# Step one's transform: products in the order of its weights, results two apart in PSUM, and a spectrum with 32 channels in a row

## The chip, the cores and the metric

The kernel runs on one core of one Trainium2 chip. The metric is the device time of one execution in microseconds (us); lower is better. The core has five engines with queues of their own: TensorE (PE, with its weight loads shown apart as PEld), VectorE (DVE), ScalarE (ACT), GpSimd (POOL) and SyncE (SP, which here only issues transfers). SBUF is the working memory, PSUM the memory into which TensorE writes its products; both have 128 partitions. All numbers in this kernel are 32-bit floats of 4 bytes.

## The reference, cut to what matters

```python
# x = A_q [1, 2048, 640]; sa, ca, ga, sb, cb, gb = parts of silu(c) @ w_mod
def _A_ref(q, k, v, shift_k, ssm_k, ssm_D):
    k_pad = jnp.pad(k, ((0, 0), (ks - 1, 0), (0, 0)))
    for t in range(ks):                       # ks = 4: short convolution
        k_shift = k_shift + k_pad[:, t:t + S, :] * shift_k[:, ks - 1 - t][None, None, :]
    kv = k_shift * v
    # long causal convolution of kv with ssm_k, channel by channel, by FFT of length 2 S
    y = irfft(rfft(kv padded) * rfft(ssm_k padded))[:S]
    y = y + kv * ssm_D[None, None, :]
    return q * y

h = _layernorm(x, axis=-1) * (1 + ca) + sa
x = x + ga * _A_ref(h, A_k, A_v, A_shift_k, A_ssm_k, A_ssm_D)
h = _layernorm(x, axis=-1) * (1 + cb) + sb
x = x + gb * _B_ref(h, B_w1, B_b1, B_w2, B_b2)   # MLP across the 2048 tokens
```

S is 2048 tokens and D is 640 channels. The change touches the first half alone, the long convolution inside `_A_ref`.

## The kernel before

**Two halves.** From the start to about 310 us the kernel computes the first half, by channels: five blocks `c` of 128 channels (`DC`, `NC`). The rest of the span is the token MLP, matrix products of 320 columns (lines 432, 1026, 951), which the change doesn't touch.

**One block of channels.** A block holds 128 channels as 2 times 64 (the two halves of the partitions, `h`), and the 2048 tokens as 64 times 32 (`n1` times `n2`). The transform over tokens is made in two steps, with matrices as constants.

- *The short convolution* (`kv_ops`, in four groups `g` of 8 `n2`): multiplications and additions, mostly on DVE, with one group in three of the first blocks on POOL. The last operation multiplies by `v` and writes the product tile `X`, 128 x 2048. Before the change X lies in the order (n2, channel): the 64 channels of one `n2` in a row. The block after the present one is convolved while the present one is transformed (the list `fill`, taken off by `dv(n)`).
- *The filter* comes by transfer into `KSR` (tile `aux`), and `perm` on ACT brings it into `KSP` (tile `p`), where the 64 values of one pair of channels lie in a row.
- *Step one* (`step1(side, t)`, matmuls at line 218): side 0 is X, side 1 is the filter. A call takes 8 pairs of channels, each with two matmuls (`ri`, real and imaginary, into the two halves of the partitions of PSUM). The pair's 128 x 64 values are the weights, and the constant `F1`, 128 columns, is the moving operand. For the filter these weights lie in a row; for X they are 32 elements (128 bytes) apart. Each matmul writes 128 columns in a row to PSUM. ACT then moves the call's 1024 columns to the spectrum `Z` (tile `z`, line 220). A block has four calls for each side.
- *Step two* (`f2(g)`, matmuls at line 234, eight calls of 32 matmuls in a block): weights from the constant `W2`, 64 in a row; the moving operand is one frequency's 64 columns of `Z`, which lie as 32 runs of two elements, 256 elements (1024 bytes) apart. ACT copies the filter's half (line 238), DVE multiplies (two operations), POOL adds into `Y`.
- *The way back*: `i2` (line 263; ACT moves the results to `T2` by line 271), `i1` (line 282; its moving operand is read from `T2` in runs of two elements, 512 bytes apart), then `gate` on DVE and POOL.

**What sets the order.** The order on every engine is the order in which the program is written (`manual_schedule`). PE's results go to a ring of three PSUM tiles of 1024 columns (`psum`), so a call can start when the third last has been read out. In blocks 1 to 3 the calls for the next block's X stand between this block's `i2` and `i1`, and those for the next filter after the first `i1`. Two matmuls that write different halves of the partitions can run at one time.

A 32-bit matmul is two instructions on PE, each with a weight load of its own, so a call of step one shows as 32 matmuls and 32 weight loads, and a call of step two as 64.

## Time and profile before

| | |
|---|---|
| median of 3 runs | 719.09 us (716.91 to 719.27) |
| the profiled execution | 718.91 us, of which the profiled span is 716.8 us |
| mean granted TensorE clock | 0.985 of full speed |
| PE busy | 646.4 us, 90% of the span |
| DVE, ACT, POOL busy | 487.0, 296.9, 118.4 us |
| step one, matmuls on X | 640 instructions, 44.8 us busy |
| step one, matmuls on the filter | 640 instructions, 39.4 us busy |
| step two, matmuls | 2560 instructions, 95.7 us busy |
| ACT, PSUM to spectrum | 40 instructions of 1140 ns |

The span is what lies between the first and the last instruction of the profile; the execution's own time is 2.1 us longer. Matmuls overlap, so an instruction's mean duration is longer than the distance from one to the next; the distance is busy time through count. Of a wait the profile names the releaser that came last.

### The profile page before, as it was taken

Reading aid. Unit: us, or ns where it says so; the run is one execution under the profiler, and the core shown is the slowest. Engines: PE = TensorE matmul, PEld = TensorE weight load, DVE = VectorE, ACT = ScalarE, POOL = GpSimd, SP = SyncE. Lnnn points to the kernel's source line nnn. Section 1 sums busy time; section 2 is a strip of 40 time slices with the busy share of each in tenths; the row PEclk is TensorE's granted clock in tenths of the full one; section 3 lists DMA queues with packets and bytes.
Section 4 is the critical chain, followed back from the end, with each engine's and each line's share of the span. In section 5 each row is a group of like instructions: output and inputs, shape, how many; then the busy total and the mean of one; then the engine's idle time right before and its main releaser. Section 6 shows DMA issues by size and latency. Waiting matters only on the chain.

```text
span 716.8 us, 20779 instructions
## 1 busy us (share of the span) xinstructions
PE 646.4 (90%) x9131; PEld 624.4 (87%) x9131; DVE 487.0 (68%) x861; ACT 296.9 (41%) x465; POOL 118.4 (17%) x135
## 2 busy tenths in 40 slices
PE   0699677989999989988799999999999989999997
PEld 0699457989999979777799999999999989999997
DVE  7768448969879538888885223112489778888887
ACT  0534373645745636456666223113244222333231
POOL 5183028414324126000110000000000000000000
PEclk9999999999999999999999999999999999999999
DMA  9978988527243522361203633443253523455510
GB/s 184 242 222 229 387 150 165 131 47 158 54 84 90 169 62 63 112 149 31 59 1 59 118 60 60 91 86 59 75 169 104 152 89 122 129 167 168 157 48 37
DMA packets 167184, 84.90 MB, mean 118 GB/s; under 512 B 89235, under 2 KB 157622, under 8 KB 167094
## 3 DMA queue, kind: packets, MB, share of 16 engines
q1 hardware_dynamic: 162546, 82.27, 45.5%
q10 hardware_dynamic: 4548, 1.31, 1.1%
q8 instruction: 71, 1.16, 0.7%
q14 instruction: 19, 0.16, 0.1%
HBM read 73.07 MB, written 10.49 MB: 117 GB/s over the span
## 4 chain that ended last, share of the span: by engine, by line
PE 54%; DVE 22%; DMA 8%; ACT 5%; SPq 5%; issue 4%; POOL 0%; ACTq 0%; DVEq 0%
PE pst L432 21%; PE pst L234 9%; PE pst L218 8%; PE pst L1026 7%; PE pst L263 4%; DVE m_w L59 4%; SPq L495 3%; DVE m_x L59 3%; PE pst L282 2%; DMA aux<-in_A_ssm_k_dram 2%; ACT m_w L939 2%; PE pst L951 2%; DMA aux<-in_w_mod_dram 2%; DVE m_x L960 1%; DVE m_v L59 1%
## 5 line engine op out<-in xcount | busy, mean ns | idle before, releaser
L234 PEld LDWEIGHTS pst<-z,w 128*64 128x64 f32 x2560 | 94.7, 141 | 7.7 <-ACT z L220 7.3
L234 PE MATMUL pst<-z,w 128*64 128x64 f32 x2560 | 95.7, 240 | 6.2 <-ACT z L220 6.1
L218 PE MATMUL pst<-v,x 128*64 128x128 f32 x640 | 44.8, 298 | 24.1 <-DVE x L59 24.0
L220 ACT ACTIVATE z<-pst 128x1024 f32<-128x1024 f32 x40 | 45.6, 1140 | 49.3 <-PE pst L218 30.2
L59 DVE TENSOR_TENSOR p<-pst,kt 128x512 f32<-128x512 f32 x80 | 51.4, 685 | 21.2 <-ACT kt L238 13.4
L218 PEld LDWEIGHTS pst<-v,x 128*64 128x64 f32 x640 | 42.8, 221 | 24.8 <-POOL t L457 23.4
L59 POOL TENSOR_TENSOR y<-p 128x256 f32<-128x256 f32 x72 | 55.2, 800 | 43.4 <-DVE p L59 43.3
L238 ACT ACTIVATE kt<-pst 128x512 f32<-128x512 f32 x40 | 25.1, 628 | 52.6 <-PE pst L234 31.9
L830 ACT ACTIVATE pst<-pst,sm 128x640 f32<-128x640 f32 x14 | 10.7, 767 | 86.0 <-PE pst L432 85.9
L951 PE MATMUL pst<-r_z,m_w 128*128 128x320 f32 x222 | 43.1, 313 | 3.0 <-DVE m_w L59 2.5
L218 PE MATMUL pst<-v,p 128*64 128x128 f32 x640 | 39.4, 281 | 6.5 <-DVE aux L59 4.6
L218 PEld LDWEIGHTS pst<-v,p 128*64 128x64 f32 x640 | 36.8, 141 | 7.8 <-DVE aux L59 4.8
L263 PEld LDWEIGHTS pst<-v,y 32*128 32x128 f32 x1280 | 37.7, 187 | 3.1 <-issue 1.6
L939 ACT ACTIVATE m_w<-m_v 128x896 fp32r<-128x896 f32 x24 | 22.1, 948 | 42.8 <-DVE m_v L59 31.0
L263 PE MATMUL pst<-v,y 32*128 32x64 f32 x1280 | 39.2, 272 | 0.6 <-ACT z L220 0.6
L951 PEld LDWEIGHTS pst<-r_z,m_w 128*128 128x128 f32 x222 | 34.8, 188 | 4.9 <-DVE m_w L59 4.0
L59 DVE TENSOR_TENSOR tap<-tap,kt 128x512 f32<-128x512 f32 x51 | 35.5, 696 | 1.3
L59 DVE TENSOR_TENSOR kt<-in,tap 128x512 f32<-128x512 f32 x51 | 35.0, 686 | 1.4
L59 DVE TENSOR_TENSOR m_w<-m_v,m_w 128x896 fp32r<-128x896 f32 x24 | 26.0, 1087 | 10.5 <-ACT m_w L939 10.5
L282 PEld LDWEIGHTS pst<-z,v 64*64 64x64 f32 x1280 | 24.8, 158 | 7.6 <-issue 4.3
L282 PE MATMUL pst<-z,v 64*64 64x64 f32 x1280 | 26.5, 244 | 5.2 <-issue 2.9
L939 ACT ACTIVATE m_w<-m_p 128x896 fp32r<-128x896 f32 x12 | 11.4, 952 | 47.1 <-DVE m_p L59 40.7
(277 smaller groups left out, 1421.0 us busy)
## 6 DMA issues: line engine op xcount, KB each, us to landing
x<-in_B_w_dram SPq DMA_DIRECT2D x22, 512.0 KB
m_v<-in_B_w_dram SPq DMA_DIRECT2D x15, 384.0 KB
x<-in_B_w_dram SPq DMA_DIRECT2D x14, 384.0 KB
aux<-in_A_ssm_k_dram SPq DMA_DIRECT2D x10, 512.0 KB
in<-in_A_k_dram SPq DMA_DIRECT2D x36, 128.0 KB
in<-in_A_v_dram SPq DMA_DIRECT2D x36, 128.0 KB
m_x<-xs SPq DMA_DIRECT2D x28, 160.0 KB
out_dram<-m_x SPq DMA_DIRECT2D x28, 160.0 KB
```

The lines of the kernel that those rows point to most:

```text
L59: TT = lambda eng, o, a, b, op: eng.tensor_tensor(o, a, b, op=op)
L218: pe.matmul(ps[64 * ri:64 * ri + 64, o:o + 128], lhs, F1[:, 128 * ri:128 * ri + 128], start=True, stop=True)
L220: evac = lambda: act.activation(Z[:, side, t].rearrange("p a k e -> p e a k"), ps.rearrange("p (e a k) -> p e a k", a=8, e=2), AF.Copy)
L234: pe.matmul(ps[64 * h:64 * h + 64, o:o + 64], W2[k1 // 32][:, 2 * (k1 % 32) + ri], rhs, start=True, stop=True)
L238: act.activation(kt.rearrange("p (m i) -> p m i", i=32), pv[:, :, 1], AF.Copy)
L263: pe.matmul(pp[qd // 2][:, o:o + 64], Y[p, ri, i:i + 2].rearrange("p i k -> p (i k)"), V2[p, 64 * ri:64 * ri + 64], start=ri == 0, stop=ri ...
L282: pe.matmul(ps[64 * b:64 * b + 64, 512 * e + 64 * jj:512 * e + 64 * jj + 64], V1[p, ri, n2], T2[p, :, 32 * ri + n2], start=ri == 0, stop=r ...
L432: pe.matmul(ps[0:m, h, 0:320], w_.bitcast(F32R), r_[:, 320 * h:320 * h + 320].bitcast(F32R), start=first and i == 0, stop=last and i == 2)
L495: sync.dma_start(XH[j // 8][64 * b:64 * b + 64, j % 8], dram(q, (16 * b + j) * D, [[32 * D, 64], [1, D]]))
L939: act.activation(W[n][0].bitcast(F32R), a(w_), AF.Copy)
L951: pe.matmul(bank[n], w[:, i].bitcast(F32R), r.bitcast(F32R), start=i == 0 and k == 0, stop=i == 6 and k == 2)
L1026: pe.matmul(acc[s][:, h, 0:320], w[:, f_].bitcast(F32R), u[r + h].bitcast(F32R), start=f_ == 0 and k == 0, stop=f_ == NF - 1 and k == 2)
```

## The change

Four things are changed together; none of them adds or takes away an instruction, a transfer or a wait, and the order on every engine is the same.

- The last product of the short convolution writes X in the order (pair of channels, n2, channel of the pair), so that the weights of one call's matmul, 64 elements, lie in a row. Each write is then a run of two elements, and the next run is 64 elements (256 bytes) further. The two channels of a pair are now neighbours (2 i and 2 i + 1) where they were 32 apart, and `perm` reads the filter in this order too.
- Step one's matmuls write every second element of PSUM (`o:o + 255:2`), so that two pairs of channels interleave.
- ACT reads PSUM in a row and writes `Z` in runs of two elements, 32 elements (128 bytes) apart. Before, it read PSUM in a row too and wrote single elements 2 elements (8 bytes) apart. The constant `F1` has its columns in another order for this.
- Step two reads its 64 columns as two runs of 32 elements. The readers behind it (`T2` in `i2`, `gate`) follow the new order of channels.

```diff
-    f1 = np.zeros((2, 64, 2, 2, 64))
+    f1 = np.zeros((2, 64, 2, 64, 2))
...
-        f1[h, :, 0, h], f1[h, :, 1, h] = np.cos(a), np.sin(a)
+        f1[h, :, 0, :, h], f1[h, :, 1, :, h] = np.cos(a), np.sin(a)
...
-    Z = T_z.rearrange("p (s t a k e) -> p s t a k e", s=2, t=4, a=8, e=2)
+    Z = T_z.rearrange("p (s k t a e) -> p s t a k e", s=2, k=128, t=4, e=2)
...
     def perm(c):
         act.activation(KSP.rearrange("p i (n e) -> p i e n", e=2),
-                       KSR.rearrange("p (e i n) -> p i e n", e=2, i=32), AF.Copy)
+                       KSR.rearrange("p (i e n) -> p i e n", e=2, i=32), AF.Copy)
...
     def kv_ops(g, eng=dve):
...
+        pairs = lambda t: t.rearrange("p n (i e) -> p n i e", e=2)
...
-        ops.append(lambda: TT(eng, X.rearrange("p (n i) -> p n i", i=64)[:, 8 * g:8 * g + 8], S_,
-                              VX[:, 8 * g:8 * g + 8], ALU.mult))
+        ops.append(lambda: TT(eng, X.rearrange("p (i n e) -> p n i e", i=32, e=2)[:, 8 * g:8 * g + 8],
+                              pairs(S_), pairs(VX[:, 8 * g:8 * g + 8]), ALU.mult))
...
     def step1(side, t, later=False):
...
-            lhs = KSP[:, i] if side else X.rearrange("p (m i) -> p i m", i=32)[:, i]
-            o = 512 * (a % 2) + 128 * (a // 2)
+            lhs = KSP[:, i] if side else X.rearrange("p (i m) -> p i m", i=32)[:, i]
+            o = 256 * (a // 2) + a % 2
             for ri in range(2):
-                pe.matmul(ps[64 * ri:64 * ri + 64, o:o + 128], lhs, F1[:, 128 * ri:128 * ri + 128], start=True,
+                pe.matmul(ps[64 * ri:64 * ri + 64, o:o + 255:2], lhs, F1[:, 128 * ri:128 * ri + 128], start=True,
                           stop=True)
-        evac = lambda: act.activation(Z[:, side, t].rearrange("p a k e -> p e a k"),
-                                      ps.rearrange("p (e a k) -> p e a k", a=8, e=2), AF.Copy)
+        evac = lambda: act.activation(Z[:, side, t], ps.rearrange("p (a k e) -> p a k e", a=4, e=2), AF.Copy)
...
     def f2(g):
...
-                    rhs = bass.AP(tensor=T_z.tensor, offset=T_z.offset + 128 * h + 2 * k1,
-                                  ap=[T_z.ap[0], [256, 32], [1, 2]])
+                    rhs = bass.AP(tensor=T_z.tensor, offset=T_z.offset + 64 * k1 + 32 * h,
+                                  ap=[T_z.ap[0], [4096, 2], [1, 32]])
...
     def i2(r, eng=None):
...
-            o = T2[:, 8 * qd + 4 * r:8 * qd + 4 * r + 4].rearrange("p a m e -> p a e m")
-            i = pp[qd // 2][:, 512 * (qd % 2):512 * (qd % 2) + 512].rearrange("p (a e m) -> p a e m", a=4, e=2)
+            a = 16 * (qd // 2) + 8 * r
+            o = T2[:, a:a + 8, :, qd % 2]
+            i = pp[qd // 2][:, 512 * (qd % 2):512 * (qd % 2) + 512].rearrange("p (a m) -> p a m", a=8)
...
     def gate(c, ps, half, eng=pool, j0=0, j1=8, then=()):
...
-        av = a.rearrange("p j (m e) -> p e j m", e=2)
-        TT(dve, av, ps.rearrange("p (e j m) -> p e j m", e=2, j=8)[:, :, j0:j1], av, ALU.mult)
+        av = a.rearrange("p j (y e c) -> p e (j y) c", e=2, c=2)
+        TT(dve, av, ps.rearrange("p (e y c) -> p e y c", e=2, c=2)[:, :, 32 * j0:32 * j1], av, ALU.mult)
```

## The prediction, as it was put on record before the changed kernel ran

> **What bounds the kernel now.** I read the chain of waits first, for where a faster or slower step would move the end. Its columns are start, length (us) and what ran.
>
> ```profile
> 70.93 11.49 DMA aux<-in_w_mod_dram
> 82.46 1.31 PE tap L342 x12
> 84.48 14.87 DMA aux<-in_A_ssm_k_dram
> ...
> 111.01 5.41 PE pst L218 x64
> 116.44 1.10 ACT z L220
> ...
> 137.19 4.27 PE pst L218 x64
> 141.46 3.73 PE pst L263 x128
> 145.19 2.24 PE pst L218 x32
> ...
> 161.89 5.42 PE pst L218 x96
> 167.39 1.09 ACT z L220
> 168.53 19.03 PE pst L234 x507
> ```
>
> Up to 111 us the end hangs on transfers (the rows of 11.49 and 14.87 us). From there to about 300 us it runs through PE: step one (L218), one ACT copy (L220), step two (L234), the way back (L263, L282), block after block. The windows confirm it (length, PE, PEld, DVE, ACT, POOL busy, granted clock, DMA share, GB/s):
>
> ```profile
> 60.20:82.50 22.30, 16.83 (x284) 13.56 (x287) 18.39 (x56) 10.50 (x14) 3.47 (x5) 0.92 0.93 304
> 111.00:116.40 5.40, 5.38 (x64) 5.14 (x64) 5.16 (x8) 1.12 (x1) 5.17 (x5) 0.68 0.94 164
> 116.40:137.20 20.80, 19.48 (x514) 19.14 (x514) 18.37 (x30) 10.88 (x22) 13.38 (x15) 1.00 0.68 149
> 167.40:187.60 20.20, 19.07 (x515) 19.08 (x517) 17.34 (x28) 10.83 (x22) 10.83 (x16) 1.00 0.57 134
> 187.60:215.60 28.00, 27.90 (x769) 26.85 (x766) 21.97 (x27) 16.52 (x20) 5.49 (x4) 1.00 0.36 67
> 265.70:285.90 20.20, 19.08 (x515) 19.00 (x518) 14.82 (x46) 11.28 (x26) 10.23 (x14) 1.00 0.30 78
> ```
>
> In 187.6 to 215.6, where most of step one stands, PE is busy 27.90 of 28.00 us: what a call of step one gains or loses there, the kernel gains or loses. Of 40 calls the path holds 26: two of the filter at 111.0, then in each of blocks 1 to 3 four on X and four on the filter (12 X, 14 filter). The first twelve lie before 70 us, beside the transfers.
>
> **Term 1, X's weights in a row.** The groups by line (busy us, mean ns of one, idle before):
>
> ```profile
> L218 PEld LDWEIGHTS pst<-v,x 128*64 128x64 f32 x640 | 42.8, 221 | 24.8 <-POOL t L457 23.4 <-POOL y L59 0.6 <-issue 0.2
> L218 PEld LDWEIGHTS pst<-v,p 128*64 128x64 f32 x640 | 36.8, 141 | 7.8 <-DVE aux L59 4.8 <-issue 1.8 <-ACT p L164 0.8
> ```
>
> The same 64 weights take 221 ns from X, 128 bytes apart, and 141 ns from the filter, in a row. How much of it counts is read from the pace of the calls, whose ends are the ACT copies that wait for them (first and last of four on X, then on the filter):
>
> ```profile
> 26.96 1.19 ACT L220 ACTIVATE z<-pst 128x1024 f32<-128x1024 f32 x1 [2.44 <-PE pst L218]
> 32.99 1.14 ACT L220 ACTIVATE z<-pst 128x1024 f32<-128x1024 f32 x1 [0.83 <-PE pst L218]
> 34.74 1.12 ACT L220 ACTIVATE z<-pst 128x1024 f32<-128x1024 f32 x1 [0.61 <-PE pst L218]
> 39.98 1.08 ACT L220 ACTIVATE z<-pst 128x1024 f32<-128x1024 f32 x1 [0.60 <-PE pst L218]
> ```
>
> X: (32.99 - 26.96) / 3 = 2.01 us a call. Filter: (39.98 - 34.74) / 3 = 1.75 us, or 54.6 ns for each of 32 instructions. With its weights in a row a call on X should go at the filter's pace: 0.26 us less, times 12 on the path = **-3.2 us**. The eight before 70 us gain nothing.
>
> The Trainium skill (SBUF — State Buffer, Specifications) gives SBUF lines of 16 bytes of which two elements must be hit for full rate. The two weight loads agree: one element in a line is the slow one.
>
> **Term 2, PSUM in steps of two.** No matmul of this trace writes PSUM in steps, so the price has to be bounded. The nearest rows are other engines' writes in the same 8-byte steps, into SBUF, and the pace of another matmul:
>
> ```profile
> L271 ACT ACTIVATE z<-pst 128x512 f32<-128x512 f32 x38 | 21.3, 666 | 19.8 <-PE pst L263 19.8
> L238 ACT ACTIVATE kt<-pst 128x512 f32<-128x512 f32 x40 | 25.1, 628 | 52.6 <-PE pst L234 31.9 <-ACT aux L289 15.3 <-ACT x L527 2.7
> L269 DVE TENSOR_SCALAR z<-pst 128x512 f32<-128x512 f32 x2 | 1.3, 686 | 0.8 <-PE pst L263 0.8
> L59 DVE TENSOR_TENSOR p<-pst,kt 128x512 f32<-128x512 f32 x80 | 51.4, 685 | 21.2 <-ACT kt L238 13.4 <-POOL y L59 7.7
> L432 PE MATMUL pst<-r_z,wb1b 128*128 128x320 f32 x180 | 28.0, 309 | 0.0
> ```
>
> ACT pays 6% for 8-byte steps (666 against 628 ns), DVE nothing (686 against 685). On PE, L432 delivers 320 columns in 28.0 / 180 = 156 ns, 0.49 ns a column; step one keeps both halves of the array going, a matmul of 128 columns per half every 2 x 54.6 = 109 ns, 0.85 ns a column. If a stepped write goes at half the rate that L432 shows, 0.97 ns, a call takes 1.75 x 0.97 / 0.85 = 2.00 us: nothing gained on X, and 14 x 0.25 = 3.5 us lost on the filter. If it is no slower than 0.85 ns, nothing is lost. The lower end is zero, since a scattered write has no reason to be quicker; a loss of more is rival one. I take **0**, because the pace needed is already below what the path delivers elsewhere; own upper end +6.7 us on term 1 (3.2 not gained, 3.5 lost).
>
> **Term 3, step two reads runs of 32.** Is step two slow because of its runs of two?
>
> ```profile
> L234 PEld LDWEIGHTS pst<-z,w 128*64 128x64 f32 x2560 | 94.7, 141 | 7.7 <-ACT z L220 7.3 <-issue 0.3
> 203.84 2.03 PE pst L282 x125
> ```
>
> It goes at 19.03 us / 512 = 37.2 ns, so 74.4 ns for 64 columns in each half. L282 also reads 64 columns in runs of two, now in four quarters: 2.03 us / 128 = 15.9 ns, 63.4 ns a quarter. So runs of two don't force more than 63.4. And weight loads can bind: L263 moves 64 columns too, but loads 128 in a row, and takes 3.73 us / 128 = 29.1, 116.6 ns a quarter. Half the load would bind at some 58 ns, with switching not far from 74. So I hold the loads, which stay as they are, for the bound: **0**. Most that could be gained: rival two.
>
> **Term 4, what gets scattered.** ACT's copy to the spectrum now writes pairs 128 bytes apart instead of elements 8 bytes apart; DVE's product writes pairs 256 bytes apart instead of a row.
>
> ```profile
> L220 ACT ACTIVATE z<-pst 128x1024 f32<-128x1024 f32 x40 | 45.6, 1140 | 49.3 <-PE pst L218 30.2 <-PE pst L282 19.0
> L421 ACT ACTIVATE wb0b<-x 128x1024 fp32r<-128x1024 f32 x10 | 10.0, 1050 | 2.2 <-PE pst L432 2.2
> L170 ACT ACTIVATE tap<-rows 128x256 f32<-128x256 f32 x3 | 2.0, 661 | 0.0
> L59 DVE TENSOR_TENSOR x<-tap,in 128x512 f32<-128x512 f32 x17 | 11.8, 692 | 10.9 <-PE pst L218 10.5
> L59 DVE TENSOR_TENSOR y<-p 128x256 f32<-128x256 f32 x8 | 4.3, 619 | 0.0
> 16.87 0.70 DVE x L59
> 126.06 0.71 DVE x L59
> ```
>
> L421 writes 1024 in a row in 1050 ns: lower end -0.1 us. With L238 (512 in 628) that is 0.82 ns an element, so 256 would be 417; L170, which reads singles 16 bytes apart, takes 661, about 1 ns an element more. At worst 1140 becomes 2100. Between, I stay at 1140, since pairs reached now and before share a line in both forms. It stands bare on the path only as the last copy before step two (4 times); elsewhere a call's 1.75 us covers it up to about that length. For DVE, L59 y<-p writes singles 256 bytes apart: 619 for 256, against 692 / 2 = 346 for as many in a row. So the product takes 692 to 2 x 619 = 1240; I take 0.8 us, nearer the row because of the pairs. On the chain it stands twice (126.06, and once at 16.9): **+0.2 us**. The other 15 lie beside PE, and the three on POOL end long before their readers. `perm`, `gate` and the copies of L271 keep their element counts and steps of 8 bytes: 0. No wait is added and no instruction moves.
>
> **Sum.** The profiled execution took 718.91 us (span 716.8 and 2.1 around it), 0.2 under the median of 719.09. 718.9 - 3.2 + 0.2 = **716 us**, by itself from 713 to 720.
>
> **Rival one: the stepped write halves PE's pace in step one.** Every matmul of it then streams twice as long, 218 ns a half, 3.49 us a call, and the weight loads vanish behind it. On the path 14 x 1.75 + 12 x (3.49 - 2.01) = 42.3 us. The first twelve calls grow by 4 x 1.75 + 8 x 1.48 = 18.8 us, of which the idle 5.5 us of PE in 60.2 to 82.5 absorb a part, before L342 at 82.46, which releases the transfer of 14.87 us: +13. The two calls at 111.0 ran at clock 0.68, so may lose up to 3 less. About **772 us**. For it: single elements reached alone do cost double where the trace shows them (L170, X's weights), and a 32-bit column may be written more than once. Against: ACT and DVE write such steps nearly free. It decides as soon as the stepped call takes over 2.1 us.
>
> The Trainium skill says just this: PSUM has lines of 8 bytes, and any pattern that isn't contiguous slows matmuls significantly (PSUM — Partial Sum Buffer, Specifications (TRN2)). No row here has a stepped matmul write, so the trace neither agrees nor disagrees; by the page this rival would be the forecast, and by the rows above term 2 is nil.
>
> **Rival two: step two speeds up.** If it reached L282's pace, 74.4 to 63.4 ns, a block would gain 256 x 11 ns = 2.8 us. DVE is busy 18.37 of 20.8 us in block 1 and 17.34 of 20.2 in 2, so I allow 1 us in block 1 and 2.8 in blocks 2, 3 and 4: -9.4, **706.5 us**. For it: 74.4 is above 2 x 54.6 / 2. Against: L282's equal runs.
>
> **Rival three: ACT's scattered copy grows to about 2.1 us.** Then it is 1.0 us more bare four times, and in blocks 1 to 3 three filter calls in a row wait for it at 0.35 us each: +4 + 3 = 7, **723 us**. It decides from about 1.8 us on, where term 1 is used up. Against: pairs, and ACT's 6% at L271.
>
> **How the numbers follow.** Forecast 0.40, rival one 0.33, rival two 0.15, rival three 0.12. About 0.3%, 2.2 us, can be told from no change. Of the forecast's 0.40, 0.27 are faster by more, 0.11 within, 0.02 slower; rival two is all faster; rival three gives 0.02 within and 0.10 slower; rival one is all slower. Together faster 0.42, within 0.13, slower 0.45. The likeliest single outcome is 716 (713 to 720); to hold 8 in 10 the range must take in rival two and the lower half of rival one: 705 to 770.
>
> **What would show it.** Right: weight loads of X near 141 ns, calls on X at 1.75 us, filter calls still 1.75, step two still 19 us a block, L220 near 1.14 us. Wrong: filter calls of 2 us and more (rival one, up to 3.5), step two under 17.5 us (rival two), L220 over 1.8 us (rival three). Rival one would make the forecast wrong by far the most.

## The result, and the profile after

| | before | after |
|---|---|---|
| median (lowest to highest) | 718.17 us (716.91 to 719.27), 4 runs | 709.57 us (706.43 to 711.1), 4 runs |
| after / before, 95% interval | | 0.9869 (0.9842 to 0.9895) |
| the profiled execution, and its span | 718.91, 716.8 us | 711.1, 709.0 us |

The medians lie 8.6 us apart, and the ratio puts the gain at 1.3%. The forecast was 716 us, 2.9 less than before. The sign is right, and the time lies in the wide range of 705 to 770 us, but it lies below the 713 to 720 that the forecast allowed itself: the gain is three times the one that was reckoned.

The page of the changed kernel, its busy times and its chain by engine:

```profile
PE 626.0 (88%) x9131; PEld 601.8 (85%) x9131; DVE 485.8 (69%) x861; ACT 291.7 (41%) x465; POOL 113.9 (16%) x135
PE 47%; DVE 27%; SPq 7%; ACT 6%; DMA 6%; issue 6%; POOL 1%; ACTq 0%; DVEq 0%; POOLq 0%
```

PE's busy time fell by 20.4 us, from 646.4 to 626.0. Its share of the chain fell from 54% to 47%, and DVE's rose from 22% to 27%. The groups by line say where on PE (busy us, mean ns, idle before). Step two before:

```profile
L234 PE MATMUL pst<-z,w 128*64 128x64 f32 x2560 | 95.7, 240 | 6.2 <-ACT z L220 6.1
```

And after, with the other groups that the change touches:

```profile
L234 PE MATMUL pst<-z,w 128*64 128x64 f32 x2560 | 79.3, 223 | 14.8 <-issue 6.3 <-ACT z L221 5.7 <-DVE p L59 2.8
L221 ACT ACTIVATE z<-pst 128x1024 f32<-128x1024 f32 x40 | 42.8, 1073 | 48.1 <-PE pst L219 48.0
L219 PE MATMUL pst<-v,p 128*64 128x128 f32 x640 | 39.1, 281 | 8.7 <-DVE aux L59 5.2 <-ACT p L164 2.5 <-issue 1.0
L219 PE MATMUL pst<-v,x 128*64 128x128 f32 x640 | 39.0, 280 | 24.7 <-DVE x L59 24.1 <-DVE p L59 0.4 <-issue 0.2
L219 PEld LDWEIGHTS pst<-v,x 128*64 128x64 f32 x640 | 36.4, 141 | 27.1 <-POOL t L458 23.5 <-issue 2.6 <-POOL y L59 0.7
L59 DVE TENSOR_TENSOR x<-tap,in 128x512 f32<-128x512 f32 x17 | 11.7, 689 | 7.9 <-PE pst L219 7.5
```

Step two, for which a gain of 0 was forecast, lost most: 95.7 to 79.3 us. Step one on X went from 44.8 to 39.0 us, now equal to the filter's 39.1, and its weight loads from 221 to 141 ns. The ACT copy is a little shorter (1140 to 1073 ns), and DVE's product, with its writes 256 bytes apart, takes 689 ns where it took 692.

The timeline of ACT over the first calls (start, length, what it did, the wait before it), first and last call on X, then on the filter:

```profile
26.95 1.10 ACT L221 ACTIVATE z<-pst 128x1024 f32<-128x1024 f32 x1 [2.51 <-PE pst L219]
32.19 1.08 ACT L221 ACTIVATE z<-pst 128x1024 f32<-128x1024 f32 x1 [0.65 <-PE pst L219]
33.93 1.10 ACT L221 ACTIVATE z<-pst 128x1024 f32<-128x1024 f32 x1 [0.67 <-PE pst L219]
39.17 1.04 ACT L221 ACTIVATE z<-pst 128x1024 f32<-128x1024 f32 x1 [0.60 <-PE pst L219]
```

X: (32.19 - 26.95) / 3 = 1.75 us a call, where it was 2.01. The filter: (39.17 - 33.93) / 3 = 1.75 us, as before. So the stepped write to PSUM costs nothing here, and X gained all that was forecast for a call.

The windows of step two on the path (length, PE, PEld, DVE, ACT, POOL busy, granted clock, DMA share, GB/s), cut here at its first and last matmul. Before, block 2, of four alike (the others are 19.70, 19.10 and 19.10 us long, with PE busy 19.48, 19.06 and 19.08):

```profile
168.50:187.50 19.00, 18.97 (x514) 18.98 (x516) 16.31 (x26) 9.76 (x21) 10.73 (x15) 1.00 0.54 126
```

And after, blocks 1 to 4:

```profile
118.30:137.30 19.00, 16.23 (x512) 15.61 (x512) 17.26 (x28) 9.57 (x22) 11.83 (x15) 1.00 0.78 170
167.70:184.30 16.60, 15.49 (x514) 15.22 (x516) 15.80 (x26) 9.57 (x22) 9.39 (x15) 1.00 0.57 132
213.00:230.40 17.40, 15.68 (x514) 15.31 (x516) 15.95 (x26) 9.53 (x21) 10.59 (x16) 1.00 0.40 116
260.30:278.40 18.10, 15.81 (x514) 15.45 (x516) 14.63 (x46) 9.90 (x25) 9.49 (x14) 1.00 0.45 131
```

Before, PE left almost nothing of these stages idle (18.97 of 19.00 us). After, it is busy 15.5 to 16.2 us in each and idle for the rest, while DVE is busy 15.80 of 16.60 us in block 2. The stages became 0.7, 2.4, 1.7 and 1.0 us shorter, 5.8 us together, though PE had 3.2 to 3.5 us less to do in each, 13.4 us together. The rest of the account, from the same kind of windows: the three stages with step one and the way back -0.9, -0.5 and -1.1, together -2.5; the two calls ahead of the first step two -0.1; the stretch from 84 us to them +0.9; the last stretch -0.5. Sum from 84 us to the end of the first half: -8.0, of the span's -7.8.

Who keeps PE waiting now is read in its timeline, block 1 (each row is a run of matmuls; in brackets the wait ahead of it and its releaser):

```profile
118.39 8.25 PE L234 MATMUL pst<-z,w 128*64 128x64 f32 x269 [1.15 <-ACT z L221]
...
132.33 2.09 PE L234 MATMUL pst<-z,w 128*64 128x64 f32 x64 [1.16 <-DVE p L59]
```

From the sixth call on, step two waits for DVE's products (p), which empty its PSUM tiles. Before, the same 512 instructions ran in one piece:

```profile
117.58 19.61 PE L234 MATMUL pst<-z,w 128*64 128x64 f32 x512 [1.19 <-ACT z L220]
```

In block 2 the profile names no releaser for PE's two pauses inside step two (0.64 and 0.38 us, "issue"), so this trace alone doesn't show DVE as their cause; an experiment below bears on it. In block 4 the chain shows what stands between DVE's products though DVE has the least to do there: layer norm statistics, which come between them in DVE's order.

```profile
263.15 1.29 DVE p L59 x2
264.44 1.35 DVE sm L510 x7
```

### The profile page after: what moved, and what is told of

It is laid out like the page before. It is cut to its first block, busy times and chain, and to the rows that moved or that the text cites. A ratio compares the mean times of both kernels' runs of the same rounds, so it can differ in the third digit from the quotient of the medians.

```text
span 709.0 us, 20770 instructions
## 1 busy us (share of the span) xinstructions
PE 626.0 (88%) x9131; PEld 601.8 (85%) x9131; DVE 485.8 (69%) x861; ACT 291.7 (41%) x465; POOL 113.9 (16%) x135
## 4 chain that ended last, share of the span: by engine, by line
PE 47%; DVE 27%; SPq 7%; ACT 6%; DMA 6%; issue 6%; POOL 1%; ACTq 0%; DVEq 0%; POOLq 0%
PE pst L433 21%; PE pst L1027 7%; PE pst L219 5%; PE pst L263 4%; DVE m_w L59 4%; PE pst L234 4%; SPq L496 3%; DVE m_x L59 3%; DVE tap L59 2%; DVE p L59 2%; DVE kt L59 2%; PE pst L283 2%; ACT m_w L940 2%; PE pst L952 2%; SPq L152 2%
## 5 line engine op out<-in xcount | busy, mean ns | idle before, releaser
L234 PE MATMUL pst<-z,w 128*64 128x64 f32 x2560 | 79.3, 223 | 14.8 <-issue 6.3
L234 PEld LDWEIGHTS pst<-z,w 128*64 128x64 f32 x2560 | 76.8, 138 | 16.1 <-issue 9.2
L221 ACT ACTIVATE z<-pst 128x1024 f32<-128x1024 f32 x40 | 42.8, 1073 | 48.1 <-PE pst L219 48.0
L219 PE MATMUL pst<-v,x 128*64 128x128 f32 x640 | 39.0, 280 | 24.7 <-DVE x L59 24.1
L219 PEld LDWEIGHTS pst<-v,x 128*64 128x64 f32 x640 | 36.4, 141 | 27.1 <-POOL t L458 23.5
L59 POOL TENSOR_TENSOR y<-p 128x256 f32<-128x256 f32 x72 | 51.1, 744 | 38.8 <-DVE p L59 38.6
L219 PE MATMUL pst<-v,p 128*64 128x128 f32 x640 | 39.1, 281 | 8.7 <-DVE aux L59 5.2
L219 PEld LDWEIGHTS pst<-v,p 128*64 128x64 f32 x640 | 36.6, 141 | 9.9 <-DVE aux L59 5.4
L238 ACT ACTIVATE kt<-pst 128x512 f32<-128x512 f32 x40 | 23.9, 598 | 46.7 <-PE pst L234 32.9
L263 PEld LDWEIGHTS pst<-v,y 32*128 32x128 f32 x1280 | 38.0, 187 | 3.8 <-issue 2.6
L263 PE MATMUL pst<-v,y 32*128 32x64 f32 x1280 | 39.9, 272 | 0.7 <-ACT z L221 0.6
L940 ACT ACTIVATE m_w<-m_v 128x896 fp32r<-128x896 f32 x24 | 22.1, 949 | 42.7 <-DVE m_v L59 30.9
L283 PEld LDWEIGHTS pst<-z,v 64*64 64x64 f32 x1280 | 24.0, 154 | 7.2 <-issue 3.1
L283 PE MATMUL pst<-z,v 64*64 64x64 f32 x1280 | 25.7, 240 | 4.6 <-issue 1.9
```

The costliest lines, as they stand in the source:

```text
L59: TT = lambda eng, o, a, b, op: eng.tensor_tensor(o, a, b, op=op)
L219: pe.matmul(ps[64 * ri:64 * ri + 64, o:o + 255:2], lhs, F1[:, 128 * ri:128 * ri + 128], start=True, stop=True)
L221: evac = lambda: act.activation(Z[:, side, t], ps.rearrange("p (a k e) -> p a k e", a=4, e=2), AF.Copy)
L234: pe.matmul(ps[64 * h:64 * h + 64, o:o + 64], W2[k1 // 32][:, 2 * (k1 % 32) + ri], rhs, start=True, stop=True)
L238: act.activation(kt.rearrange("p (m i) -> p m i", i=32), pv[:, :, 1], AF.Copy)
L263: pe.matmul(pp[qd // 2][:, o:o + 64], Y[p, ri, i:i + 2].rearrange("p i k -> p (i k)"), V2[p, 64 * ri:64 * ri + 64], start=ri == 0, stop=ri ...
```

## The experiments

Every ratio is to the kernel before, run on the same chip in the same rounds.

### The two halves of the change

The spectrum alone (kernel before, and of the change only F1's order, the stepped PSUM, the copy and step two's runs of 32):

```diff
-    Z = T_z.rearrange("p (s t a k e) -> p s t a k e", s=2, t=4, a=8, e=2)
+    Z = T_z.rearrange("p (s k t a e) -> p s t a k e", s=2, k=128, t=4, e=2)
...
-                pe.matmul(ps[64 * ri:64 * ri + 64, o:o + 128], lhs, F1[:, 128 * ri:128 * ri + 128], start=True,
+                pe.matmul(ps[64 * ri:64 * ri + 64, o:o + 255:2], lhs, F1[:, 128 * ri:128 * ri + 128], start=True,
...
-                                  ap=[T_z.ap[0], [256, 32], [1, 2]])
+                                  ap=[T_z.ap[0], [4096, 2], [1, 32]])
```

> Only the spectrum's part: PSUM in steps of two, the copy to the spectrum in pairs, step two reading 32 in a row; X stays as before. Theory (step two was bound by reading its 64 columns in runs of two): step two's 2560 matmuls take 79 us busy instead of 95.7, calls on X stay at 2.0 us, time 5 to 7 us under before. Rival (step two got faster because the calls around it did, not by its own reading): step two stays near 95 us and the time within 2 us of before.

The order of X alone (the changed kernel with those edits taken back):

```diff
-                                  ap=[T_z.ap[0], [4096, 2], [1, 32]])
+                                  ap=[T_z.ap[0], [256, 32], [1, 2]])
```

> Only the order of X: the product written so that step one's weights lie in a row; PSUM, spectrum and step two as before. Theory: calls on X at 1.75 us instead of 2.01, step two unchanged at 95.7 us busy, time 2.5 to 3.2 us under before (12 calls of 0.26 us on the path), and the two parts add up to the whole change (8.6 to 9.4 us). Rival (the two parts need each other): less than 1 us here.

Measured: the spectrum alone 711.96 us (709.68 to 715.69), ratio 0.9936 (0.9901 to 0.9971); the order of X alone 715.66 us (710.88 to 719.7), ratio 0.9976 (0.9945 to 1.0006). The groups by line of the first:

```profile
L233 PE MATMUL pst<-z,w 128*64 128x64 f32 x2560 | 79.0, 223 | 12.5 <-ACT z L220 5.7 <-issue 4.2 <-DVE p L59 2.4
L218 PE MATMUL pst<-v,x 128*64 128x128 f32 x640 | 45.2, 300 | 24.7 <-DVE x L59 24.3 <-DVE p L59 0.4
L220 ACT ACTIVATE z<-pst 128x1024 f32<-128x1024 f32 x40 | 42.6, 1065 | 52.3 <-PE pst L218 51.9
```

And of the second:

```profile
L235 PE MATMUL pst<-z,w 128*64 128x64 f32 x2560 | 95.6, 240 | 6.2 <-ACT z L221 6.1
L219 PE MATMUL pst<-v,x 128*64 128x128 f32 x640 | 39.4, 282 | 24.4 <-DVE x L59 23.8 <-DVE p L59 0.3 <-issue 0.3
```

The busy times separate cleanly. The spectrum alone gives step two its 79 us and the copy its 1065 ns, and leaves X at 45.2; the order of X alone gives 39.4 on X and leaves step two at 95.6. Of the times, only the first lies clear of no change; the second's interval just reaches it. Both gains are smaller than was expected of them (4.6 us by the ratio where 5 to 7 were expected, 1.7 where 2.5 to 3.2 were), and together they make 0.9% where the whole change makes 1.3%; the intervals are wide enough for that, so these two runs don't show that the parts add up. The stepped PSUM is in the first alone, and the calls on the filter are no longer for it.

### Is it the run of two?

Step two of the changed kernel reads its columns as runs of two again, but near each other (16 bytes from run to run), and both halves read the same columns; the way back (L283) reads 64 in a row. What it computes is therefore not the convolution.

```diff
-                    rhs = bass.AP(tensor=T_z.tensor, offset=T_z.offset + 64 * k1 + 32 * h,
-                                  ap=[T_z.ap[0], [4096, 2], [1, 32]])
+                    rhs = bass.AP(tensor=T_z.tensor, offset=T_z.offset + 64 * k1,
+                                  ap=[T_z.ap[0], [4096, 2], [4, 16], [1, 2]])
...
-                                  V1[p, ri, n2], T2[p, :, 32 * ri + n2], start=ri == 0, stop=ri == 1)
+                                  V1[p, ri, n2], T_z[p, 4096 + 64 * (32 * ri + n2):4160 + 64 * (32 * ri + n2)], start=ri == 0, stop=ri == 1)
```

> The changed kernel, where step two reads 64 other columns: runs of two elements 16 bytes apart (two blocks 16 KB apart), and the way back's last step (64 columns from T2) reads 64 in a row instead of runs of two 512 bytes apart; what is computed is no longer the convolution. Theory one (what costs is the run of two, wherever the next one lies): step two back to 37 ns an instruction. Theory two (what costs is the wide step of 1024 bytes): step two stays at 30 to 31 ns. For the last step: if runs of two cost there as well, it goes from 15.9 ns an instruction in its stretches to 14.5 or less; if not, it stays.

One run took 707.88 us. Its groups by line:

```profile
L234 PE MATMUL pst<-z,w 128*64 128x64 f32 x2560 | 79.0, 220 | 11.9 <-ACT z L221 5.7 <-issue 3.4 <-DVE p L59 2.7
L283 PE MATMUL pst<-z,v 64*64 64x64 f32 x1280 | 24.1, 228 | 5.0 <-issue 3.2 <-ACT z L272 0.9 <-ACT g L361 0.8
```

Runs of two cost step two nothing here (79.0 us against the changed kernel's 79.3), and the way back gains little by reading in a row (24.1 against 25.7). So the length of a run by itself isn't what made step two slow.

### Prices of reads and of stepped writes, by themselves

Groups of 32 to 64 instructions that nothing reads are added to the changed kernel after the first half: 32 matmuls of 256 columns at a time, writing PSUM in a row or by steps of two, in 16 and in 32 bits; then matmuls of 64 columns in two halves, and in four quarters, that read in a row, in pairs and in single elements.

```diff
+    each(32, lambda i: pe.matmul(acc[0][:, i % 2, 0:256], HB(bw)[:, 0:128], HB(bm[:, 0:256])[:, 0:256], **GO))
+    each(32, lambda i: pe.matmul(acc[0][:, i % 2, 0:511:2], HB(bw)[:, 0:128], HB(bm[:, 0:256])[:, 0:256], **GO))
+    each(32, lambda i: pe.matmul(acc[0][:, i % 2, 0:256], bw, bm[:, 0:256], **GO))
+    each(32, lambda i: pe.matmul(acc[0][:, i % 2, 0:511:2], bw, bm[:, 0:256], **GO))
...
+    each(32, lambda i: pe.matmul(out2(i), bw[:, 0:64], pairs_(32, 4)[:, :, 0:2], **GO))
...
+    each(32, lambda i: pe.matmul(out2(i), bw[:, 0:64], pairs_(64, 2)[:, :, 0], **GO))
+    each(32, lambda i: pe.matmul(out2(i), bw[:, 0:64], pairs_(64, 16)[:, :, 0], **GO))
...
```

> The changed kernel with 13 groups of 32 extra matmuls beside its 24 warming ones, into a PSUM tile that is overwritten after; only the distance between matmuls in each group is of interest. PSUM in steps of two: theory (a 32-bit matmul delivers a column only every 0.83 ns in its part of the array, and PSUM takes a lone column in that time): 256 columns of 32 bits go alike in a row and in steps, some 108 ns an instruction twice over, while 256 columns of 16 bits, one every 0.42 ns, take 110 to 130 ns in a row and about 215 ns in steps. Rival: 16 bits go alike in a row and in steps too. Reading 64 columns of 32 bits with both halves of the array at work: in a row 30 ns an instruction; runs of two at 16 and at 128 bytes 37 ns each by theory one (the run), 30 and more by theory two (only wide steps cost); runs of four 30; single elements 45 or more at 64 bytes. In quarters: in a row and runs of two both about 16 ns, singles 25 or more.

The whole kernel took 754.29 us with them. The chain of waits through the groups (start, length, line; in this order 16 bits in a row, 16 bits stepped, 32 bits in a row, 32 bits stepped, then pairs 16 bytes apart, single elements 8 bytes apart and single elements 64 bytes apart):

```profile
308.10 3.51 PE pst L786 x32
311.61 6.91 PE pst L787 x32
318.51 13.81 PE pst L788 x64
332.33 13.81 PE pst L789 x64
...
348.16 1.87 PE pst L791 x64
...
353.98 1.87 PE pst L794 x64
355.85 3.54 PE pst L795 x64
```

In 16 bits a stepped write takes twice the time: 6.91 / 32 = 216 ns an instruction against 110 ns. In 32 bits it is the same to the last digit: 13.81 / 64 = 216 ns in both forms. All three are 216 / 256 = 0.84 ns a column, which is also the pace of step one (0.85 ns by the prediction's own division). So a stepped column takes about 0.84 ns, and each of the two instructions of a plain 32-bit matmul takes as long for a column in a row.

The Trainium skill says that any pattern that isn't contiguous slows matmuls significantly (PSUM — Partial Sum Buffer, Specifications (TRN2)). The 16-bit groups agree, 110 to 216 ns; the 32-bit ones don't, 216 and 216 ns, and the measurement decides: for the matmuls of this change the rule has no price.

Of the reads by two halves, pairs cost 1.87 / 64 = 29 ns an instruction, single elements 8 bytes apart the same, and single elements 64 bytes apart 3.54 / 64 = 55 ns. In quarters, as on the way back, pairs cost nothing either (L797, 1.02 us for the group, against L796, 1.09 us in a row). All reads of these groups go by steps of 256 bytes or less, and both halves read the same place; step two's old reads go by steps of 1024 bytes, its halves in different places.

### Where the two halves read

So groups were put behind the first step two of the changed kernel, that read the spectrum itself, step two's way: matmuls of 64 columns, alternating between the halves, with the pattern of reading (the length of a run, the step between runs and the distance between the halves' places) as the only thing that varies. There are two runs of this kind. The first mainly varies the step, mostly with the halves 512 bytes apart as in the kernel before:

```diff
+                    mv_ = bass.AP(tensor=T_z.tensor, offset=T_z.offset + apart * h, ap=[T_z.ap[0]] + ap)
...
+            for o_, w_, m_v in each([[256, 32], [1, 2]], 128):
+                pe.matmul(o_, w_, m_v, start=True, stop=True)
...
+            for o_, w_, m_v in each([[256, 32], [1, 2]], 16):
+                pe.matmul(o_, w_, m_v, start=True, stop=True)
```

> The changed kernel with 14 groups of 64 extra matmul instructions (32 matmuls of 64 columns in 32 bits, halves of the array in turn, weights of step two) between step two and step one of the first block, reading the spectrum in different patterns into a PSUM tile that nothing reads; only the distance within a group is of interest. In a row, both halves from one place or 512 bytes apart: 30 ns. Runs of two 1024 bytes apart, halves 512 bytes apart (step two before): 37 ns, if the old pattern alone was the cause. Theory two (a step of 1024 bytes is slow by itself): also 37 with both halves from one place, and with 1008 bytes (a step that is no power of two); 34 at 512, 32 at 128 bytes, 29 to 30 at 16 bytes; runs of four at 1024 bytes 31 to 34. Theory three (the two halves collide because they are 512 bytes apart): 30 with both halves from one place or 64 bytes apart. Theory four (powers of two collide in the memory): 30 with the step of 1008 bytes. Single elements at 64 bytes 55, at 16 bytes 45 to 55.

One run took 736.1 us with the groups. Its chain of waits (64 instructions a group; L563 is exactly the old step two):

```profile
63.63 2.34 PE pst L563 x48
65.97 2.35 PE pst L565 x48
68.32 1.87 PE pst L567 x64
70.18 2.37 PE pst L569 x61
72.55 2.35 PE pst L571 x64
74.89 2.00 PE pst L573 x61
76.90 1.87 PE pst L575 x64
...
82.66 1.91 PE pst L579 x64
```

L563, pairs 1024 bytes from one to the next, halves 512 bytes apart: 2.34 us / 64 = 36.6 ns, the old pace of step two (37.2). L565, the same with both halves at one place: 36.7. L567, the same with the halves 64 bytes apart: 29.2, free. L569 and L571, steps of 512 bytes (halves 256 apart) and of 256 (halves 512 apart): 37.0 and 36.7. L573, step 128: 31.3. L575, step 64: 29.2. L579, step 1008 bytes, which is nearly as far as the slow one but walks off the multiples of 256: 29.8. Columns in a row don't pay for halves 512 bytes apart: the mean of one is 223 ns (L561) against 222 with both halves at one place (L559), where the slow groups show 240. All these groups ran at a granted clock of 1.00.

The second varies the distance between the halves, at the step of 1024 bytes:

> As the last bench of reading patterns, in the changed kernel: runs of two 1024 bytes apart, the second half's columns 16, 32, 64, 128, 256, 768 and 960 bytes from the first half's; runs of four 1024 bytes apart, both halves from one place or 64 bytes apart; single elements 32 bytes apart from one place, 256 bytes apart from one place and 64 bytes apart. Theory (two streams collide when they stand on the same place modulo 256 bytes or less): 37 ns at 256 and 768 bytes, 29 to 30 ns at 64, 128 and 960; 16 and 32 bytes tell how fine the places are. Rival (only an offset of 64 bytes helped by chance, or the start of a group): no order by distance. Single elements 55 to 58 ns from one place.

One run took 729.86 us. Its groups by line (64 instructions each; mean ns of one, where matmuls overlap). The halves are 16, 32, 64, 128, 256, 768 and 960 bytes apart in the lines 559 to 571:

```profile
L567 PE MATMUL pst<-z,w 128*64 128x64 f32 x64 | 2.5, 240 | 0.0
...
L565 PE MATMUL pst<-z,w 128*64 128x64 f32 x64 | 2.2, 220 | 0.1
...
L571 PE MATMUL pst<-z,w 128*64 128x64 f32 x64 | 2.0, 220 | 0.0
```

Only 256 and 768 bytes (L567, L569) show 240 ns, the figure of the kernel before; 16, 32, 64, 128 and 960 show 219 to 220. With the first run's 0 and 512, the distances that cost, of the nine tried, are those that are multiples of 256 bytes, at steps that are multiples of 256 too; a distance of 1024 has no result. Runs of four, 1024 bytes apart, hardly pay: 1.98 / 64 = 30.9 ns with both halves at one place (L573), 29.2 with them 64 bytes apart (L575). So it takes short runs as well. Single elements of this run, from its chain of waits (256 bytes from one to the next, halves at one place, then 64 bytes apart):

```profile
81.95 4.68 PE pst L579 x64
86.63 3.54 PE pst L581 x64
```

4.68 / 64 = 73 ns against 55 ns: single elements this far apart are slow for themselves, and with the shared place they are slower still. (The first 3 us of L579 had a granted clock of 0.50 to 0.64 and the rest 1.00; its instructions start every 73 ns in both.)

The Trainium skill has the 16-byte lines of SBUF, of which two elements must be hit (SBUF — State Buffer, Specifications). The single elements agree: 55 ns 64 bytes apart, against 29 for pairs and 29 for single elements 8 bytes apart, of which two lie in a line.

### The old layout with the halves parted

If that is the cause, the kernel before must gain as much with no new layout: its second half takes the same eight frequencies of a call in another order, four places on, which puts the halves 32 bytes apart modulo 256. It also moves the places in PSUM that the two halves write at one time; the groups above kept those places alike in both halves, fast or slow.

```diff
-            k1 = 8 * g + kk
             for ri in range(2):
                 for h in range(2):
-                    o = 128 * kk + 64 * ri
+                    kh = kk ^ 4 * h
+                    k1, o = 8 * g + kh, 128 * kh + 64 * ri
```

> The kernel before, with one edit: in step two the second half of the array takes the eight frequencies of a call in another order (four places on), so that the two halves, which work at one time, read addresses 32 bytes off each other's steps; layout, PSUM and counts as before. Theory (the two halves collide when their runs fall on the same place of a 256-byte pattern): step two 79 us busy at 31 ns an instruction and a time 4 to 6 us under before, as with the spectrum's part alone. Rival (32 bytes are too few, or the collision needs more than order): step two stays at 95 us, no change.

Measured: 711.79 us (706.07 to 715.8), ratio 0.9919 (0.9885 to 0.9952). Its group of step two:

```profile
L234 PE MATMUL pst<-z,w 128*64 128x64 f32 x2560 | 79.3, 220 | 12.2 <-ACT z L220 6.1 <-issue 3.8 <-DVE p L59 2.1
```

79.3 us busy, the changed kernel's number, with runs of two 1024 bytes apart and PSUM written in a row. Then the same edit together with the new order of X, without the new spectrum:

> The order of X as in the changed kernel and, in place of the new spectrum, only the other order of frequencies in the second half: PSUM in a row, the spectrum's layout as before, step two still in runs of two. Theory (the new layout gains by parting the two halves' reads, and nothing else of it matters): step two 79 us busy, calls on X 1.75 us, a time like the changed kernel's, ratio 0.985 to 0.991. Rival (the pairs in a row or the copy's shorter time, 1073 for 1140 ns, add something of their own): 2 us and more slower than the changed kernel, ratio over 0.991.

Measured: 707.88 us (704.41 to 709.97), ratio 0.9866 (0.9836 to 0.9895), and its groups by line:

```profile
L235 PE MATMUL pst<-z,w 128*64 128x64 f32 x2560 | 78.5, 220 | 11.0 <-ACT z L221 6.1 <-DVE p L59 3.3 <-issue 1.6
L221 ACT ACTIVATE z<-pst 128x1024 f32<-128x1024 f32 x40 | 45.2, 1132 | 47.1 <-PE pst L219 29.1 <-PE pst L284 17.8
```

The ratio is the changed kernel's (0.9869): two lines in step two and the order of X give all of its gain. The stepped PSUM, the new order of F1 and the runs of 32 have none of their own that shows; even the shorter ACT copy (1132 here, 1073 there) brings nothing that can be told.

### Why step two's gain came through by half

PE's work in step two fell by 13.4 us on the path and the stages by 5.8. If DVE is what is late, the gap must vanish when DVE has less to do. Both kernels were run without six of the seven operations that come before the product with `v` in the short convolution, wherever they run (mostly DVE), so that neither computes the reference:

```diff
-        for s in (2, 1, 0):
+        for s in ():
             ops.append(lambda s=s: TT(eng, T_, kx(s), w(s), ALU.mult))
```

> The kernel before with six of the seven preparatory operations of each short convolution left out (only the first tap and the product with v remain), so DVE and POOL have far less beside step two. If PE bounds the blocks before, as the chain said: step two still 19 us a block, time 0 to 8 us under before, the most of it at the start, where the first products wait for these operations.

> The changed kernel with the same operations left out. Theory (what was gained on PE was given back to waits for DVE, which is busy with the short convolution in the same stretches): step two falls to 15.5 to 16.5 us in blocks 1 to 3, and the distance to cut_before grows from the 8.6 to 9.4 us of the whole kernels to 12 to 16 us. Rival (the rest is lost to PE's own order, or to ACT and POOL): the distance stays at 8 to 10 us and step two at 16.6 to 19 us.

Measured: the kernel before, cut, 718.29 us (713.66 to 720.93), ratio 1.0011 (0.998 to 1.0042); the changed one, cut, 704.08 us (700.78 to 706.2), ratio 0.9813 (0.9749 to 0.9876). Step two of the cut changed kernel, in PE's timeline, block 2 and the second half of block 3:

```profile
165.39 15.15 PE L234 MATMUL pst<-z,w 128*64 128x64 f32 x512 [1.12 <-ACT z L221]
...
218.49 7.74 PE L234 MATMUL pst<-z,w 128*64 128x64 f32 x256 [1.51 <-DVE p L59]
```

And of the cut kernel before, in the chain of waits:

```profile
167.79 19.03 PE pst L234 x506
```

Before, less work on DVE is worth nothing: step two keeps its 19.03 us. After, block 2 runs in one piece of 15.15 us, 29.6 ns an instruction, so the pauses that the profile gave no releaser went with DVE's work. The kernels now lie 718.29 - 704.08 = 14.2 us apart instead of 8.6, by 5.6 us more; the intervals leave about 5 us either way to that. The stages of step two are the closer measure. In the changed kernel the cut takes them from 71.1 us to 15.84 + 14.98 + 16.74 + 17.84 = 65.4, which is 5.7 us less; in the kernel before, from 76.9 to 77.3 (19.05, 19.02, 20.11 and 19.09, from the first matmul of step two to the next line's). So 5 to 6 us of the gain had gone into waits that DVE's convolution made. Block 3 still waits 1.51 us once, and the kernel before, cut, pauses at the same place (0.86 us, for ACT): the cut doesn't free all of it.

Two attempts to take that work off DVE without leaving it out. First, one group of the convolution of the last two blocks on POOL:

```diff
+            pool.tensor_scalar(PW, TR.rearrange("p (i s) -> p s i", s=4), 1.0, None, op0=ALU.mult)
...
+                run(kv_ops(2, pool))
-                fill.extend(kv(c + 3 if c + 3 < NC else None))
+                fill.extend(kv(c + 3 if c + 3 < NC else None, ((0,), (1, 2), (3,))))
```

> The changed kernel with one group of four of the short convolution for blocks 3 and 4 moved from DVE to POOL (seven operations each, 1.35 us instead of 0.7), placed after step two, where POOL was nearly idle. Theory: DVE has 5 us less a block, step two in blocks 2 and 3 falls by 1 to 2 us each: 2 to 4 us under the changed kernel, a ratio to before of 0.982 to 0.985. Rival (POOL slows DVE by reading beside it, or POOL's product comes late): equal to the changed kernel or slower, 0.987 to 0.995.

Then, in the changed kernel, one addition of 2048 elements per block, in blocks 1 to 3, on POOL instead of DVE:

```diff
-        po = [lambda: TT(dve, A1, A1, g(G1), ALU.mult), lambda: TT(dve, A1, A1, g(G0), ALU.add)]
+        po = [lambda: TT(dve, A1, A1, g(G1), ALU.mult), lambda: TT(pool, A1, A1, g(G0), ALU.add)]
```

> The changed kernel with one of DVE's two long operations of 2.3 us in blocks 1 to 3 (the addition of the shift to the normalized queries) moved to POOL, which is idle there. Theory (DVE is what step two waits for in these blocks): 1 to 4 us under the changed kernel, a ratio to before of 0.981 to 0.986. Rival (POOL's operation, 4.8 us or more, comes late for the gate or holds DVE): 0.987 or more.

The first made it slower: 730.86 us (728.36 to 733.18), ratio 1.0201 (1.0142 to 1.026). Step one waits for POOL, as its group shows. The chain of waits of this kernel shows POOL's operations at two lengths, and its timeline shows what DVE runs beside the long ones:

```profile
L219 PE MATMUL pst<-v,x 128*64 128x128 f32 x640 | 43.5, 300 | 45.1 <-DVE x L59 24.4 <-POOL x L59 19.8 <-issue 0.5
```

```profile
142.82 1.28 POOL t L59
...
144.17 3.22 POOL t L59
```

```profile
143.98 5.55 DVE L59 TENSOR_TENSOR aux<-aux,g 128x2048 f32<-128x2048 f32 x2
```

There are 19.8 us of waits for POOL's X, and an operation of 1.28 us takes 3.22 at times. The long ones lie beside DVE's two operations of 2048 elements, which take 5.55 us here and 4.61 us in the kernel before. Beside DVE's convolution, just ahead, POOL's took 1.28 us and DVE's their 0.7. That the two engines hold each other up there is argued from these times, not tested. The second brought nothing: 710.22 us (708.83 to 714.23), ratio 0.9916 (0.9884 to 0.9948), which overlaps the changed kernel's. The moved addition takes 4530 ns on POOL and 2285 on DVE. So the work isn't moved to POOL for free, and no version that computes the reference beats the changed kernel by more than the intervals.

## Why the prediction was right in its sign and wrong in its size

**Term 1, X's weights in a row: right.** 1.75 us a call as forecast, weight loads at 141 ns, and X alone takes 39.4 us without the rest of the change. The three stages that hold these calls became 2.5 us shorter, beside the 3.2 foretold; alone, the edit measured -0.24%, 1.7 us, not clear of no change.

**Term 2, the stepped PSUM: right, at zero.** The filter's calls kept 1.75 us. The prediction argued from the pace needed, 0.85 ns a column, and the matmuls by themselves bore that out: a stepped column takes 0.84 ns. Its bound of 0.97 ns, made from twice L432's 0.49, came out near the measured 0.84 but was taken from another kind of matmul: the program hands L432 its numbers as `float32r`, one instruction a matmul, where step one's plain 32-bit matmul is two. A column in 0.49 ns was never within step one's reach, so that row couldn't show that the path delivers faster. Rival one's doubling does happen, to a matmul as quick as the 16-bit one, 110 / 256 = 0.43 ns a column. Its own support was weaker than it said: by its rows single elements cost not double but 1.6 times (221 against 141 ns, 661 against 417).

**Term 3, step two: wrong, and this is the step that failed.** The prediction took L282 as proof that runs of two cost nothing much, and was right in that. From there it went to the weight loads as the bound: it halved L263's 116.6 ns to some 58, gave the rest up to 74 to a "switching" for which it had no row, and put the gain at zero. The loads stayed as they are (141 ns before, 138 after), and step two went from 37.2 to 29.6 ns an instruction all the same, under the 31.7 that L282's pace stood for. At 29.6 a half takes 59.2 ns, close to that 58; whether the loads bind it there, no run shows. What made L234 slow was a third thing: where the two halves read. The old step two's halves read 512 bytes apart, at steps of 1024, and the new one's 128 bytes apart and in a row. By the program's text L282's two halves read 128 bytes apart, which cost nothing at a step of 1024; that this is why it wasn't slow is argued from that group, not shown on L282 itself.

**Rival two was what happened, with its size nearly right for another reason.** The prediction gave it 0.15, and the measured time lies within 705 to 770 only because that range took it in; with the forecast's mechanism that is luck. It foretold -9.4 us on step two beside the forecast's own -3. It allowed 1 us in block 1 and 2.8 in each of blocks 2 to 4; measured were 0.7, 2.4, 1.7 and 1.0. PE's own gain was larger than it reckoned (up to 3.9 us a block, 19.03 to 15.15), and DVE let less of it through. The prediction saw this cover in block 1 (DVE busy 18.37 of 20.8 us) and took the other blocks as free, at 17.34 of 20.2; with PE down to 16.2, 15.5 and 15.7 us in blocks 1 to 3, DVE's work there of 17.3, 15.8 and 16.0 us is the longer of the two.

**Term 4, the scattered writes: no cost.** The product's writes in pairs 256 bytes apart took 689 ns, not the 0.8 us that was taken. The copy got faster, 1140 to 1073 ns, in the spectrum-only kernel too (1065) and not with the order of X alone (1132): rival three had the wrong sign.

Sum, with the measured terms on the path: step one -2.5, step two -5.8, the rest +0.5: -7.8 us in the span, where the prediction had -3.2 + 0 + 0.2.

## What to carry to other kernels

Where two matmuls run at one time in different parts of the array, compare the places that their moving operands read at the same moment, not only the pattern of one: two streams of two-element runs, with steps of a multiple of 256 bytes and a distance of such a multiple, cost 37 ns where 29 was possible, and another order of the same work parts them. Before a gain on the bounding engine is booked in full, put the busy time of the next engine in that same stage beside the new length, block by block; here 7.6 of 13.4 us didn't come through, and most of that went to waits that ended when DVE had less to do. Before a row is taken for a pace, look whether it is the same kind of instruction. When two rows differ in speed, list all that differs between them (addresses too) before one difference is named the bound.

## What the runs showed of the hardware that was not expected

- Two concurrent 64-column matmuls that read SBUF in pairs of elements: 36.6 to 37 ns an instruction where step and distance are multiples of 256 bytes (steps of 256, 512 and 1024; distances 0, 256 and 512), 29.2 with the halves 64 bytes apart, 29.8 with a step of 1008 bytes. Columns in a row and runs of four hardly pay (223 against 222 ns of mean length, 30.9 against 29.2 ns an instruction). Which part of the memory the two streams share isn't shown by any run.
- A matmul's write to PSUM by steps of two takes 0.84 ns a column: 216 against 110 ns for 256 columns in 16 bits, and 216 against 216 ns for each instruction in 32 bits.
- Operations that no edit touched became a little shorter in the changed kernel: ACT's copy of the filter's half (L238) 628 to 598 ns, and POOL's additions into `Y` 800 to 744 ns. They go with step two's pace and not with the layout: 601 and 758 ns in the kernel before with its halves parted, 627 and 810 ns with the order of X alone. What links them was not tried.
